# One kernel, a new opening: unit 0's v on another queue, weights behind a small write, products of zeros, and a new order of steps

## The chip, the cores and the metric

The kernel runs on one core of a Trainium2 chip. The core has five engines with an instruction queue each: TensorE (PE, matrix products, with its weight loads shown as PEld), VectorE (DVE), ScalarE (ACT), GpSimd (POOL) and SyncE (SP, which here only issues transfers). Transfers can be issued from SP, ACT and POOL; their packets are moved by 16 DMA engines that all queues share. Engines take their instructions strictly in the order of their own queue and wait for each other by semaphores.

The metric is device time in microseconds (us). The kernel before took 236.48 us, the median of 4 runs (235.59 to 236.83).

## The reference

For 4 batches, 8 heads, 768 time steps and a head size of 48, a gated linear recurrence and then a network with a rational activation:

```python
f = 1.0 / (1.0 + np.exp(-f_logit))
for t in range(S):
    state = f[:, :, t, :, None] * state + np.einsum('bhd,bhe->bhde', k[:, :, t], v[:, :, t])
    y[:, :, t] = np.einsum('bhd,bhde->bhe', q[:, :, t], state)
x = y.transpose(0, 2, 1, 3).reshape(B * S, H * D)      # 3072 x 384
h = x @ w_in                                           # 384 x 2048
P = a[0] + a[1] * h + a[2] * h * h + a[3] * h ** 3
Q = 1.0 + abs(b[0]) * abs(h) + abs(b[1]) * h * h
out = (P / (Q + 1e-6)) @ w_out                         # 2048 x 384
```

Inputs and the output are float32.

## The kernel before, in words

The work is cut into 12 units. Unit n is chunk n // 4 of 256 time steps and batch n % 4, with all 8 heads; units 0 to 3 are the first chunk, whose state starts at zero. A unit's 256 steps are two blocks (j = 0, 1) of 128.

The order of everything is written out by hand in one table, the string ORDER. Each entry names a step, its unit and its arguments; the program runs through the table once and issues what each step issues. So each engine's queue is the table filtered to that engine. A step that waits holds up all later steps of its engine. There is no scheduler behind the table. A number after @ names one of four PSUM slots, which the step takes over from its previous user, and for which it waits.

The steps of a unit, first the recurrence:

- `ld` loads f, k, q or v. f, k and q go through SP's queue in float32; v goes through POOL's queue, which converts it to bfloat16 on the way. Unit 0's f, k and q are loaded in two halves of four heads (arguments 2 4 and 0 2), the others in one piece. SP's transfers land in the order of issue.
- `ef`, `ls` (ACT): exp and log that make -log f. `cs` (PE): sums of it over time, by products with triangles of ones. `A` (ACT, line 312): the two exponentials of the sums; `xa` (DVE, line 317): q and k times them. `T` (PE, line 328) and `Te` (DVE, line 336): transposition and the copy out of PSUM.
- `sc` (PE, line 349) and `mk` (DVE, line 357): the masked scores of keys and queries. `ya` (PE): what the state gives to y, and the update of the state, which needs v; `ae` (ACT) and `st` (DVE): the new state. `vm` (line 364): two small copies of v into a padded tile. `yb` (PE, line 370): scores times v. `ye` (ACT, line 420): y out of PSUM.

Then the network, in groups of 128 of the 2048 columns, 0 to 16 (`h 0 4 8` is unit 0, groups 4 to 7):

- `h` (PE, line 438): y times w_in; `hy` (ACT, line 452): h to bfloat16; `ab` (DVE): its absolute value; `sq` (DVE) or `sa` (ACT): its square.
- Q: either `u` (PE, line 472), which adds the two terms by products with an identity, and `ln` (ACT, line 480) on the result in PSUM; or the sum in place by a DMA of POOL that accumulates (`zd`, line 489) or by DVE (`zv`), and `lz` (ACT, line 496) on the result. `ex` (ACT, line 504): 1/Q as the exponential of minus the logarithm.
- P: `p1`, `p2`, `pm` (DVE), and its last sum by an accumulating DMA of POOL (`ta`, line 523) or by DVE (`tv`). `gm` (DVE, line 532): P/Q.
- `o` (PE, line 539): the product with w_out; `oe` (ACT or DVE): out of PSUM; `so`, `s0`, `s1`: the store.

Once at the start: `wi` and `wo` load w_in and w_out through POOL's queue, four transfers for each `wi`, one per 32 partitions of the tile; `ab_` loads the coefficients a and b; `fa` and `fb` (DVE, lines 259 to 276) make scale factors from them, and `rg` reads two of these into registers of ACT, which `ye`, `ln` and `lz` use; `ca`, `cb`, `cc`, `cz` write constants. `zw` (zeros in a bfloat16 tile) and `wm` (products of that tile with itself into a PSUM slot that nobody reads) are defined in the program, but the table before does not use them.

In the table before, the coefficients are loaded by SP between unit 0's fourth and fifth half loads, and POOL issues v of unit 0 and then w_in's transfers as fast as it can.

## Time and profile before

One execution was profiled. It took 238.19 us, of which the program's span on the core is 236.5 us. The profile's numbers:

| engine | busy us | share of the span | instructions |
|---|---|---|---|
| PE | 215.6 | 91% | 3116 |
| DVE | 205.3 | 87% | 242 |
| ACT | 202.2 | 85% | 214 |
| POOL | 73.5 | 31% | 98 |

A line of the groups of instructions has the source line, the engine, the operation, what it writes and reads with the shape, how often, the busy time, the mean of one in ns, and the idle time of the engine just before it with what ended that. In a line of the time line, the first two numbers are the start and the duration in us; the bracket is the idle time of that engine before, and what ended it. In the table of stretches, each engine's busy us stand in the order PE, PEld, DVE, ACT, POOL, with the number of instructions, then TensorE's granted clock (1.00 is full speed), then the share of the DMA engines and the rate. In the chain of waits, a line has a start, a length and what the time went to.

A busy PE isn't PE at its peak: a product's end is modelled, and the same product takes longer with a slower clock.

### The profile page before, as it was taken

What the parts mean: (1) busy time and instruction counts of PE and PEld (TensorE: products, weight loads), DVE (VectorE), ACT (ScalarE), POOL (GpSimd) and SP (SyncE); (2) the same over time, 40 slices, a digit from 0 to 9 for tenths busy, and PEclk for the clock granted to TensorE, in tenths of its full rate; (3) what the DMA queues carried; (4) which work ended last, traced back from release to release, by engine and by line L of the source; (5) the groups of instructions that cost most, each with busy time, mean ns of one, the idle gap of its engine ahead of it and who ended that gap; (6) DMA issues with size and microseconds to landing.
All of it is one profiled execution on the core that took longest, in us unless ns stands there. A gap on an engine that the chain in (4) does not pass through costs nothing.

```text
span 236.5 us, 7112 instructions
## 1 busy us (share of the span) xinstructions
PE 215.6 (91%) x3116; PEld 148.6 (63%) x3128; DVE 205.3 (87%) x242; ACT 202.2 (85%) x214; POOL 73.5 (31%) x98
## 2 busy tenths in 40 slices
PE   1369779999999999999999999999999999999992
...
DVE  4653597899889899999999999999999799999940
ACT  5205584999997999999999999989999999899950
...
PEclk9999995999999999999999999999999999999999
...
GB/s 133 153 232 213 204 204 210 228 132 44 156 257 227 225 165 244 257 138 165 264 131 179 194 228 176 233 214 173 122 123 93 181 69 55 200 211 98 196 57 76
DMA packets 61998, 40.56 MB, mean 172 GB/s; under 512 B 51472, under 2 KB 58128, under 8 KB 61968
## 3 DMA queue, kind: packets, MB, share of 16 engines
...
q1 hardware_dynamic: 41104, 18.68, 33.1%
...
## 4 chain that ended last, share of the span: by engine, by line
PE 40%; DVE 20%; ACT 18%; DMA 12%; issue 6%; SPq 1%; DVEq 0%; POOLq 0%; ACTq 0%
PE op L539 13%; PE hp L438 12%; DMA z<-h 6%; ACT hy L452 5%; PE u L472 4%; DVE scm L357 4%; DMA kn<-in_k_dram 4%; ACT qi L504 3%; PE cs L303 3%; PE y L370 3%; ACT lq L496 2%; DVE gall L532 2%; DVE qkp L317 2%; DMA qn<-in_q_dram 2%; ACT lq L480 2%
## 5 line engine op out<-in xcount | busy, mean ns | idle before, releaser
L438 PE MATMUL hp<-xT,w_in_sb 128*128 128x256 bf16 x576 | 70.1, 278 | 1.6 <-DMA w_in_sb<-in_moe_w_in_dram 1.1
L539 PE MATMUL op<-w_out_sb,gall 128*128 128x384 bf16 x384 | 68.8, 326 | 0.6 <-DVE osb L554 0.6
L438 PEld LDWEIGHTS <-w_in_sb 128*128 128x128 bf16 x576 | 56.5, 100 | 12.1 <-issue 2.8
L452 ACT CAST hy<-hp 128x1024 bf16<-128x1024 f32 x48 | 49.3, 1067 | 4.8 <-PE hp L438 4.8
L539 PEld LDWEIGHTS <-gall 128*128 128x128 bf16 x384 | 36.4, 98 | 24.7 <-issue 1.1
L504 ACT ACTIVATE qi<-lq 128x2048 bf16<-128x2048 f32 (+1 forms) x25 | 46.8, 1879 | 0.1
L523 POOL DMA_DIRECT2D gall<-hy x21 | 18.6, 918 | 77.4 <-ACT lq L480 30.5
L532 DVE TENSOR_TENSOR gall<-gall,qi 128x2048 bf16<-128x2048 bf16 (+1 forms) x25 | 29.3, 1177 | 1.5 <-ACT qi L504 1.1
L519 DVE TENSOR_TENSOR gall<-gall,h 128x2048 bf16<-128x2048 bf16 (+1 forms) x25 | 29.2, 1175 | 0.0
L357 DVE TENSOR_TENSOR scm<-sc,mask 128x1024 bf16<-128x1024 f32 x24 | 29.0, 1215 | 0.3 <-PE sc L349 0.2
L480 ACT ACTIVATE lq<-u 128x1024 f32<-128x1024 f32 x24 | 24.6, 1050 | 1.8 <-PE u L472 1.8
L496 ACT ACTIVATE lq<-z 128x2048 f32<-128x2048 bf16 x12 | 23.6, 1969 | 1.5 <-DMA z<-h 1.5
L364 POOL COPY vmp<-vn 128x128 bf16<-128x128 bf16 x24 | 19.4, 897 | 15.8 <-PE y L370 6.3
L489 POOL DMA_DIRECT2D z<-h x9 | 12.1, 1347 | 38.4 <-DVE z L464 16.4
L456 DVE TENSOR_TENSOR h<-hy 128x2048 bf16<-128x2048 bf16 (+1 forms) x17 | 19.6, 1152 | 1.9 <-ACT hy L452 1.9
L312 ACT ACTIVATE A<-cs 128x768 f32<-128x768 f32 (+1 forms) x26 | 19.5, 800 | 1.6 <-PE cs L303 1.5
L317 DVE TENSOR_TENSOR qkp<-qn,A 128x768 bf16<-128x768 f32 (+1 forms) x13 | 11.7, 896 | 8.5 <-ACT A L312 8.1
L509 DVE TENSOR_SCALAR gall<-hy,a_sb 128x4096 bf16<-128x4096 bf16 (+2 forms) x15 | 17.1, 1140 | 2.1 <-ACT hy L452 2.1
L464 DVE TENSOR_SCALAR z<-hy 128x2048 uint16<-128x2048 uint16 (+1 forms) x25 | 17.0, 681 | 1.1 <-ACT hy L452 1.1
L460 ACT ACTIVATE h<-hp 128x1024 bf16<-128x1024 f32 x16 | 17.3, 1102 | 0.1
L303 PE MATMUL cs<-lsp,Ui 128*128 128x384 bf16 (+1 forms) x39 | 11.5, 360 | 5.9 <-ACT lsp L293 4.9
L328 PE MATMUL tp<-ident,qkp 128*128 128x128 bf16 x192 | 14.1, 227 | 3.0 <-DVE qkp L317 3.0
...
## 6 DMA issues: line engine op xcount, KB each, us to landing
...
```

What stands on the lines that cost most here:

```text
L312: nc.scalar.activation(t, src, AF.Exp, scale=1.0 if x else -1.0)
L357: nc.vector.tensor_mul(t, s["sc", g].rearrange("s r a i t -> s (r a) (i t)"), mb)
L364: nc.gpsimd.tensor_copy(s["vm"][:, :, :, 32 * x:32 * x + 16], src)
L438: nc.tensor.matmul(t[:, m - m0, :].rearrange("f (j t) -> f j t", j=UB), w_in_sb[:, kk, m * P:(m + 1) * P], s["x"][:, :, kk, :], start=(kk ...
L452: nc.scalar.copy(fl(big(s, "hy", "hy", 3), m0, m1), fl(s["hp", m0], 0, m1 - m0))
L456: nc.vector.tensor_mul(fl(big(s, "h2", "h2", 2), m0, m1), fl(s["hy"], m0, m1), fl(s["hy"], m0, m1))
L480: nc.scalar.activation(fl(s["lq", g], m0 - 8 * g, m1 - 8 * g), fl(s["u", m0], 0, m1 - m0), AF.Ln, scale=rsig2, bias=1.0 + 1e-6)
L496: nc.scalar.activation(fl(s["lq", g], m0 - 8 * g, m1 - 8 * g), fl(s["z"], m0, m1), AF.Ln, scale=rsig2, bias=1.0 + 1e-6)
L504: nc.scalar.activation(fl(s["qi", g], m0 - 8 * g, m1 - 8 * g), fl(s["lq", g], m0 - 8 * g, m1 - 8 * g), AF.Exp, scale=-1.0)
L519: nc.vector.tensor_mul(fl(s["g"], m0, m1), fl(s["g"], m0, m1), fl(s["h2"], m0, m1))
L532: nc.vector.tensor_mul(fl(s["g"], m0, m1), fl(s["g"], m0, m1), fl(s["qi", g], m0 - 8 * g, m1 - 8 * g))
L539: nc.tensor.matmul(s["op"][:, j, 0:DM], s["g"][:, m, C * j:C * j + C], w_out_sb[:, m, :], start=(m == 0), stop=(m == KF - 1))
```

## The change

The table is replaced. What it and the functions now do differently:

- Unit 0's v is loaded by SP in float32 as the seventh of its transfers, behind the six halves of f, q and k, into a tile of its own; a new step `vc` converts it on ACT. Unit 0's two `vm` copies are made by ACT. POOL loads v for the other units as before.
- The coefficients a and b are loaded through ACT's queue, at its head. `fa` and `fb` stand in DVE's queue ahead of all four of unit 0's `xa`; before, they stood between them. `rg` stands between unit 0's `A` steps.
- The half loads come as f, f, q, k, k, q; heads 4 to 7 go first through `xa`, `T` and `Te`.
- `hv` writes two zeros (bitcast to one float32) in each partition of w_in's tile, in group 0's columns, from DVE between the third and the fourth `xa` of unit 0. The load of groups 0 to 3 overwrites them, so it waits for that write, and what stands behind it in POOL's queue too: v of unit 1, groups 8 to 15 (now one `wi` with four transfers of double width), w_out. The load of groups 4 to 7 stands ahead of it and waits for nothing.
- 80 products of zeros (`wm`, 128x128 by 128x256) stand in 14 places of PE's queue, all before unit 0's `h 0 12 16`. In order of place there are 11, 1, 3, 5, 3, 6, 4, 2, 20, 5, 9, 1, 9 and 1 of them.
- After the start, the order of steps differs throughout. The set of steps is the same but for one half of a unit (8 groups), whose sum for Q is made by an accumulating DMA and one `lz`, where before two `u` and two `ln` made it: 22 `u` and `ln` instead of 24, 10 `zd` instead of 9, 13 `lz` instead of 12.

```diff
 ORDER = """
-cz 3; cb; ld 0 f 2 4; ld 0 f 0 2; ca; cz 2; ld 0 k 0 2; cz 0; ld 0 q 0 2; cz 1; ld 0 v; cc; ab_
-ef 0 2 4; wi 4 8; ls 0 2 4; ld 0 q 2 4; ef 0 0 2; cs 0 2 4 @0; ls 0 0 2; A 0 0 2 4; cs 0 0 2 @1
-ld 0 k 2 4; A 0 1 2 4; A 0 0 0 2; wi 0 4; ld 1 f; A 0 1 0 2; xa 0 0 0 2; fa; xa 0 1 0 2; rg; ld 1 q
-wi 12 16; fb; T 0 0 2 @1; xa 0 0 2 4; Te 0 0 2; ld 1 k; xa 0 1 2 4; sc 0 0 @1; ya 0 0 @0 @2; mk 0 0
-vm 0 1; ld 1 v; T 0 2 4 @3; ae 0; st 0 0; vm 0 0; Te 0 2 4; wi 8 12; ya 0 1; sc 0 1 @3; st 0 1
-yb 0 0 2; mk 0 1; ef 1; ld 2 f; ls 1; yb 0 2 4; ye 0; cs 1 @3; h 0 4 8 @0; A 1 1; A 1 0; ld 2 q
-h 0 0 4 @2; hy 0 4 8; xa 1 0; hy 0 0 4; sq 0 0 8; h 0 12 16 @2; wo 8 12; ld 2 k; xa 1 1; wo 4 8
-ab 0 0 8; wo 0 4; hy 0 12 16; T 1 @0; p1 0 0 8; wo 12 16; u 0 4 8 @3; Te 1; ef 2; ld 3 f; u 0 0 4 @2
-p2 0 0 8; ln 0 4 8; ld 2 v; ya 1 0 @0 @1; pm 0 0 8; ln 0 0 4; vm 1 0; sc 1 0 @3; vm 1 1; mk 1 0
-ae 1; ls 2; sc 1 1 @2; ld 3 q; ex 0 0 8; st 1 0; cs 2 @3; mk 1 1; ya 1 1; A 2 1; tv 0 0 8; yb 1
-A 2 0; h 0 8 12 @2; st 1 1; ye 1; ld 3 k; gm 0 0 8; h 1 4 8 @0; hy 0 8 12; xa 2 0; h 1 8 12 @2
-p1 0 8 16; hy 1 4 8; sq 0 8 16; sa 1 4 8; h 1 12 16 @1; xa 2 1; hy 1 8 12; h 1 0 4 @0; pm 0 8 16
-hy 1 12 16; ld 4 f; ef 3; T 2 @2; ab 0 8 16; hy 1 0 4; sq 1 8 16; u 0 8 12 @1; sa 1 0 4
-u 0 12 16 @3; p2 0 8 16; ln 0 8 12; ab 1 0 8; o 0 0 0 4 @0; tv 0 8 16; ln 0 12 16; u 1 4 8 @1; ls 3
...
+zw; ab_; cz 2; cb; ld 0 f 2 4; ld 0 f 0 2; ca; cz 3; ld 0 q 2 4; cz 1; ld 0 k 2 4; cz 0; cc
+ld 0 k 0 2; ef 0 2 4; ls 0 2 4; ld 0 q 0 2; ef 0 0 2; fa; wm 11 @3; cs 0 2 4 @0; ls 0 0 2; ld 0 v
+A 0 0 2 4; wm 1 @3; cs 0 0 2 @1; fb; A 0 1 2 4; xa 0 0 2 4; ld 1 f; rg; xa 0 1 2 4; A 0 0 0 2
+wm 3 @3; T 0 2 4 @0; A 0 1 0 2; ld 1 k; Te 0 2 4; xa 0 1 0 2; wm 5 @3; sc 0 1 @0; ld 1 q; hv 0
+xa 0 0 0 2; wi 4 8; mk 0 1; wm 3 @3; T 0 0 2 @1; vc 0; Te 0 0 2; vm 0 1 s; wm 6 @3; ya 0 0 @0 @2
+vm 0 0 s; wi 0 4; sc 0 0 @1; ae 0; ef 1; ld 2 f; st 0 0; mk 0 0; wm 4 @3; ya 0 1; ls 1; ld 1 v
+yb 0 2 4; st 0 1; yb 0 0 2; wi 8 16; cs 1 @1; ye 0; A 1 0; wm 2 @3; h 0 4 8 @0; A 1 1; hy 0 4 8
+xa 1 1; ld 2 k; wm 20 @3; h 0 0 4 @0; xa 1 0; ld 2 q; hy 0 0 4; wm 5 @3; T 1 @1; ab 0 0 8; sq 0 0 8
+ef 2; ld 3 f; Te 1; wm 9 @3; u 0 0 4 @0; ls 2; vm 1 1; ya 1 0 @2 @3; p1 0 0 8; vm 1 0; ln 0 0 4
+ld 2 v; cs 2 @1; p2 0 0 8; ae 1; sc 1 0 @0; st 1 0; A 2 1; ld 3 k; mk 1 0; wm 1 @0; ya 1 1; A 2 0
+xa 2 1; sc 1 1 @1; u 0 4 8 @0; st 1 1; mk 1 1; ln 0 4 8; ld 3 q; pm 0 0 8; ex 0 0 8; wm 9 @3; yb 1
+wm 1 @3; h 0 12 16 @1; wo 8 12; xa 2 0; ye 1; wo 0 4; tv 0 0 8; ld 4 f; h 0 8 12 @0; ef 3; wo 4 8
+gm 0 0 8; hy 0 12 16; wo 12 16; h 1 4 8 @2; hy 0 8 12; h 1 12 16 @1; ls 3; ld 4 k; sq 0 8 16
+sa 1 4 8; vm 2 1; h 1 8 12 @0; p1 0 8 16; hy 1 12 16; ld 3 v; ab 0 8 16; hy 1 4 8; h 1 0 4 @3
+vm 2 0; pm 0 8 16; hy 1 8 12; p2 0 8 16; u 0 12 16 @2; sa 1 0 4; ld 4 q; sq 1 8 16; u 0 8 12 @0
...
-u 10 8 12 @3; ex 10 0 8; pm 10 8 16; u 11 4 8 @2; o 9 0 8 12; pm 11 0 8; ta 10 8 16; ln 10 8 12
+h 11 0 4 @2; sq 10 8 16; ln 9 12 16; o 8 1 8 12; pm 10 0 8; zd 10 8 16; o 8 1 12 16; hy 11 0 4
...
@@ -190,12 +191,25 @@
         t0 = s["c"] * NT
         src, eng, dt = {"f": (f_logit, nc.sync, F32), "k": (k, nc.sync, F32),
                         "q": (q, nc.sync, F32), "v": (v, nc.gpsimd, BF16)}[what]
+        if n == 0 and what == "v":
+
+            what, eng, dt = "v32", nc.sync, F32
+            s[what] = consts.tile([P, H, 2, D], F32, name="v32")
         if what not in s:
             s[what] = ld.tile([P, H, 2, D], dt, name=what + "n")
         hh = slice(2 * a0, 2 * a1)
         eng.dma_start(out=s[what][:, hh].rearrange("p h i d -> p h (i d)"),
                       in_=src[s["b"], hh, t0:t0 + NT, :].rearrange("h (p i) d -> p h (i d)", i=2))
 
+    def vc(n):
+        s = unit(n)
+        s["v"] = ld.tile([P, H, 2, D], BF16, name="vn")
+        nc.scalar.copy(s["v"].rearrange("p h i d -> p (h i d)"), s["v32"].rearrange("p h i d -> p (h i d)"))
+
+    def hold(m0):
+
+        nc.vector.memset(w_in_sb[:, 0, m0 * P:m0 * P + 2].bitcast(F32), 0.0)
+
     def load_w_in(m0, m1):
 
         cols = slice(m0 * P, m1 * P)
@@ -208,9 +222,9 @@
                             in_=moe_w_out[m0 * P:m1 * P, :].rearrange("(ko ki) n -> ki ko n", ki=P))
 
     def load_ab():
-        nc.sync.dma_start(out=b_sb, in_=bass.AP(tensor=moe_b.tensor, offset=moe_b.offset,
+        nc.scalar.dma_start(out=b_sb, in_=bass.AP(tensor=moe_b.tensor, offset=moe_b.offset,
                                                 ap=[[0, P]] + list(moe_b.ap)))
-        nc.sync.dma_start(out=a_sb, in_=bass.AP(tensor=moe_a.tensor, offset=moe_a.offset,
+        nc.scalar.dma_start(out=a_sb, in_=bass.AP(tensor=moe_a.tensor, offset=moe_a.offset,
                                                 ap=[[0, P]] + list(moe_a.ap)))
 
     def const_a():
@@ -356,12 +370,16 @@
         mb = _at(mask, [[0, 4], [1, 2 * C]])
         nc.vector.tensor_mul(t, s["sc", g].rearrange("s r a i t -> s (r a) (i t)"), mb)
 
-    def vm(n, x):
+    def vm(n, x, eng="g"):
 
         s = unit(n)
         vv = s["v"].rearrange("p (a r) i d -> p r i a d", r=2)
         src = vv[:, 0, :, :, 32:48] if x == 0 else vv[:, 1, :, :, 0:16]
-        nc.gpsimd.tensor_copy(s["vm"][:, :, :, 32 * x:32 * x + 16], src)
+        dst = s["vm"][:, :, :, 32 * x:32 * x + 16]
+        if eng == "s":
+            nc.scalar.copy(dst, src)
+        else:
+            nc.gpsimd.tensor_copy(dst, src)
 
 
     PIECE = ((0, 0), (0, 1), (1, 1), (1, 2))
@@ -553,7 +571,7 @@
             s["osb"] = ms.tile([P, UB, DM], F32, name="osb")
         (nc.scalar.copy if eng == "s" else nc.vector.tensor_copy)(s["osb"][:, j0:j1], s["op"][:, j0:j1, 0:DM])
 
-    steps = dict(ld=load, wi=load_w_in, wo=load_w_out, ab_=load_ab, ca=const_a, cb=const_b, cc=const_c,
+    steps = dict(ld=load, hv=hold, vc=vc, wi=load_w_in, wo=load_w_out, ab_=load_ab, ca=const_a, cb=const_b, cc=const_c,
                  cz=const_z, fa=coef_a, fb=coef_b, rg=regs, wm=wm, zw=zero_w, ef=ef, ls=ls, cs=cs, A=A, xa=xa, T=T, Te=Te,
                  sc=sc, mk=mk, vm=vm, ya=ya, yb=yb, ye=ye, ae=ae, st=st, h=h, hy=hy, sq=sq, ab=ab, u=u, ln=ln,
                  zv=zv, zd=zd, sa=sa, lz=lz, ex=ex, p1=p1, p2=p2, pm=pm, ta=ta, tv=tv, gm=gm, o=o, oe=oe, so=store,
```

## The prediction

> **What bounds the kernel now.** I read the slices of the page first, then the stretches of the start and of the middle, then the chain of waits and the time line up to 45 us.
>
> The page's slices (40 of 5.9 us each, busy tenths):
>
> ```profile
> PE   1369779999999999999999999999999999999992
> DVE  4653597899889899999999999999999799999940
> ACT  5205584999997999999999999989999999899950
> PEclk9999995999999999999999999999999999999999
> ```
>
> The stretches:
>
> ```profile
> 12.00:18.00 6.00, 4.19 (x78) 3.08 (x78) 3.05 (x5) 0.77 (x2) 5.33 (x11) 1.00 1.20 232
> 18.00:24.00 6.00, 5.65 (x93) 3.66 (x93) 1.78 (x2) 3.22 (x5) 2.98 (x5) 1.00 1.35 213
> 36.00:42.00 6.00, 6.00 (x115) 4.31 (x115) 3.93 (x5) 3.04 (x4) 0.00 (x0) 0.57 1.14 204
> 80.00:220.00 140.00, 139.06 (x2118) 98.39 (x2124) 136.63 (x141) 138.10 (x141) 44.63 (x47) 1.00 0.89 171
> ```
>
> From 80 to 220 us PE idles 0.9 us, ACT 1.9 and DVE 3.4: all three are full, and a us gained ahead of this stays gained. The slack is in the first 42 us. There, the chain of waits:
>
> ```profile
> 4.44 9.05 DMA kn<-in_k_dram
> ...
> 18.94 1.24 DVE scm L357
> ...
> 22.65 3.38 PE hp L438 x24
> ```
>
> And the time line:
>
> ```profile
> 7.89 0.17 DVE L259 TENSOR_SCALAR bm<-b_sb 128x2 uint32<-128x2 uint32 x1 [0.28 <-DMA b_sb<-in_moe_b_dram]
> ...
> 13.52 0.56 DVE L317 TENSOR_TENSOR qkp<-kn,A 128x384 bf16<-128x384 f32 x1 [1.41 <-DMA kn<-in_k_dram]
> ...
> 21.30 0.81 ACT L420 ACTIVATE xT<-y 128x768 bf16<-128x768 f32 x1 [2.17 <-PE y L370]
> ...
> 22.44 1.83 PE L438 MATMUL hp<-xT,w_in_sb 128*128 128x256 bf16 x8
> ...
> 27.12 1.47 PE L438 MATMUL hp<-xT,w_in_sb 128*128 128x256 bf16 x12 [1.10 <-DMA w_in_sb<-in_moe_w_in_dram]
> ...
> 41.28 1.01 ACT L452 CAST hy<-hp 128x1024 bf16<-128x1024 f32 x1 [1.83 <-PE hp L438]
> ...
> 43.05 1.22 DVE L456 TENSOR_TENSOR h<-hy 128x2048 bf16<-128x2048 bf16 x1
> ```
>
> The last half of k is issued at 4.44 and lands at 13.5; unit 0 ends with `ye` at 22.1. The 128x256 product takes 0.229 us at 22.44 and 0.122 at 27.12, though the granted clock is written as 1.00 in both: I read the early rows as half speed, not yet on record. It is on record for 36 to 42 us (0.57).
>
> **The change, part by part.** Landings below are issue plus time to landing.
>
> *Loads.* In SP's queue the first four half loads land at 3.6, 4.3, 5.4 and 6.0 us, then b at 7.9, a at 8.8, and the fifth and sixth half at 10.95 and 13.5. So b and a, 3 KB, stand in front of q and k for some 2.5 us, and v and seven w_in transfers of POOL run beside the last two halves. Now b and a are on ACT's queue, and POOL starts with four w_in transfers. At 0.8 us per half, six halves land by 7.6; v (two halves) by 9.2, plus four w_in transfers at 0.65 each (their landings follow each other so) 11.8. Bounds for v: 9.2 and 13.5 (the sixth half of before); I take 11.8. `vc` is a 128x768 pass on ACT, 0.84, and two `vm` there 0.2 to 0.5 each (POOL's rows 0.30): v is ready at 13.2. It is covered if `ya 0 0` can't start sooner.
>
> The Trainium skill speaks against this part: "DMA: Bandwidth & Descriptors", section "Issuing engines are not separate DMA queues", says that issuing from several engines saves only issue time. By that rule moving b and a gains about 1 us (two issues of 0.43 to 0.51). The 7.0 and 9.1 us to landing of the halves behind them, against 3.6 ahead, say more.
>
> *b at the head of DVE.* `fa` (7.89 to 9.39, 1.5 us) and `fb` (0.7) now precede all `xa`, so b's landing heads the chain. ACT issues it after its table load, at 2.1. With the 4.9 us to landing of before it is there at 7.0, with the 2.4 of ACT's store at 4.5; I take 6.0, as half of its old wait was for the loads ahead of it. ACT's two issues (0.5 each) end at 3.1, before f lands; `rg` waits for `fa` (7.5) and holds two `A` of 0.49, which end at 8.6, 2 us before their `xa`. Then `fa`, `fb` to 8.2; two `xa` of 0.56 to 9.3; `T` to 9.9; `Te` 0.69 to 10.6; two `xa` and `hv` (0.1) to 11.8; `T` 0.7 to 12.5; six zeros of 0.23 to 13.9 (covering v); `ya 0 0` 1.4 to 15.3; `ae` and `st` 0.9 to 16.2; `ya 0 1` from 16.8 (behind `sc` 0.64 and four zeros 0.9) to 18.3, with `mk` 1.22 beside it; `yb` 2.1 to 20.4; `ye` 0.8 to 21.2, against 22.1: 0.9 gained with the slow clock throughout. With the fast one after 12 us the zeros, `ya`, `yb` give up half: 0.7 + 0.7 + 0.45 + 0.7 + 1.0 = 3.5, so 4.4 gained. With half of the stretch fast, `ye` ends at 19.4 and 2.7 is gained.
>
> The zeros stand in gaps of PE; a gap that closes early turns them into a delay, 0.12 us each fast, 0.23 slow (the same shape). The skill's "TensorE: Matmul & The Clock Gate", section "The HAM clock gate (the 'warmup' mystery)", has full speed after about 3.4 us of sustained products. By that alone it would come before 12 us and the gain would be the 4.4. This trace has products for 5.65 of 6 us from 18 to 24 and yet 0.229 us at 22.44; I stay between.
>
> *From `ye` to unit 0's last square.* `A 1` two times 0.76 on ACT to 20.9; `h 0 4 8` (12 products, 1.4) on PE to 20.8; `hy` to 21.9. Then 20 zeros, 2.4 us, to 23.2, `h 0 0 4` to 24.6, `hy` to 25.6. The held w_in transfers (issued from about 11.4 to 13.7, 5.5 to 9.0 to landing as before) are in by 17 to 22.7, so the zeros, not the weights, set this. Behind them in POOL's queue stand v of unit 1 (issued at 14.5; 9.7 to landing before, so 24, wanted by `ya 1 0` at 28), and w_out behind the copies of that v (issued to 27; up to 15.5 to landing, so 42.5, wanted by `o` past 43). `ab`, `sq`, `Te 1` (0.69, 1.23, 1.22) to 28.7, against 31.65. `p1`, `p2`, `st` to 30.9, `mk` 32.1, `xa` 33.1; on PE `ya 1 1` and `sc 1 1` behind a zero that waits for that `mk`'s slot, to 33.5; `u` 0.9 to 34.4; on ACT `ln` 0.96, `ex` 1.92, `ye 1` 0.81, `ef 3` 0.85 and two `hy` to 41.0. Before, `hy 0 8 12` ends at 42.3 with `ef 3` (0.88) still to do: ACT is 2.2 ahead. `sq 0 8 16` ends at 42.2 against 44.27, with an `xa` (0.95) more and a `p1` (0.81) less behind it: DVE too is 2.2 ahead. The old slow stretch from 34 to 41 has no place in this chain: nine zeros and `yb` precede `h 0 12 16`. `ef 3` needs f of unit 3, which landed at 42.9 before and wasn't needed till 46.2; now SP's queue carries one more load but loses its block, and POOL's transfers start later. If it landed at 40 the chain would wait 2 us.
>
> *The full middle.* Two `u` and two `ln` less, one `zd` and one `lz` more. PE: 8 products of 128x512, at 0.215, are 1.7 us less. ACT: 2 x 1.05 - 1.97 = 0.1 less. POOL: 1.35 more, hidden in its 31%; the accumulation lands in 7.0. As all three engines are full, between 0.1 and 1.7 is gained; at the end PE has 8 us of `op` products without a pause from 222, so I take the middle, 0.9. The new order there can't be priced from the diff: it can save at most ACT's 1.9 us of idle time, and I let it cost up to DVE's 3.4 once more; value 0, as ends of both signs are near.
>
> Sum: 2.2 + 0.9 = 3.1. The profiled execution goes from 238.19 to 235.1; it stood 0.7% above the median, from which 236.48 - 3.1 = **233.4 us**.
>
> **Rivals.**
> - *The zeros lie on the chain and open no clock* (slower). Place: the 20 before `h 0 0 4`. At the slow clock, with `ye` at 21.2, `h` (2.75), 20 zeros (4.6) and `h` again (2.75) end at 31.5, `hy`, `ab`, `sq`, `Te` at 35.7: 4.0 behind 31.65, so 240.5 less the 0.9: 239.6. It decides if the slow clock holds beyond about 26 us. Against it: 24 `hp` products sufficed before.
> - *Held weights late* (slower). The point is 23.2, where the zeros end; each us beyond it costs one, and beyond 26.5 the start gains nothing. At 9.0 to landing they are in by 22.7. Wide transfers for groups 8 to 15 are wanted only at 35; v before had up to 16.0 to landing, from 18 at the latest: 34. A transfer 3.5 us later still: 238.
> - *The start's gain is given back* (no change): unit 3's f at 40 takes 2 of the 2.2; or a queue in the middle stands behind an accumulation not yet landed (before: 1.5 us over two such waits for `z`). 235.5 to 237.
> - *Clock open by 12 us and PE the bound*: 4.4 + 1.7 = 6.1, so 230.4.
>
> **How the numbers follow.** Forecast 0.64, open clock 0.08, given back 0.16, zeros 0.08, weights 0.04. The forecast's own range is 231.0 to 235.2. Of "given back" I count 0.02 as faster and 0.03 as slower: faster by over 0.5% (1.2 us, about what a measurement of this kernel can tell) 0.74, same 0.11, slower 0.15. The range cuts half of the fast case, and most of the two slow ones: 230.8 to 237.8.
>
> **What would show it.** b lands by 7 us, and the line 259 starts there; q and k of unit 0 land by 8, v by 12; `ye` ends between 18 and 21; the 12 products of `h 0 4 8` take about 1.4 us; `h 0 0 4` follows the zeros with no wait for w_in; ACT's `ef 1` and `ef 2` don't wait for f, and `ef 3` starts by 39; `sq 0 8 16` ends near 42; between 80 us and 217 all three engines idle as little as before. I am wrong if b lands after 8, if the first `hp` products still take 0.23, if ACT waits for f of unit 2 or 3, or if the middle shows new waits for `z` or `gall` of over 2 us.

## The result, and the profile after

The changed kernel takes as long as the kernel before: its time over that of the kernel before is 0.999, with a 95% interval from 0.9966 to 1.0013 (medians 237.67 us over 42 runs and 237.22 over 63). The forecast was 233.4 us, 3.1 less. The profiled execution went from 238.19 to 237.28 us, its span from 236.5 to 235.6. Ratios are taken over undisturbed runs only, the medians over all; the profiled execution after is 1.5% above its kernel's fastest run and so not an undisturbed one, but the start that it shows is there again in e3 and its wait for z in e6, whose profiled executions are.

The slices of the page after (40 of 5.9 us, busy tenths):

```profile
PE   5778869999999999999999999979999999999991
DVE  6573579699999979999999999979999999999960
ACT  3455257999996999999999999969999999999970
PEclk9999997999999999999999999999999999999999
```

TensorE is busier in the first three slices, which hold the zero products. PE, DVE and ACT now all have a notch in slice 27 (153 to 159 us), where PE and DVE stood at 9 and ACT at 8 before. The stretches after (columns: length, busy time of PE, its weight loads, DVE, ACT, POOL, then granted clock, DMA share, GB/s):

```profile
12.00:18.00 6.00, 4.58 (x148) 3.56 (x150) 4.47 (x6) 3.08 (x6) 4.96 (x9) 1.00 1.13 221
18.00:24.00 6.00, 5.21 (x61) 4.17 (x50) 1.93 (x3) 3.24 (x4) 0.78 (x3) 1.00 1.31 205
36.00:42.00 6.00, 6.00 (x103) 4.62 (x102) 4.63 (x5) 5.11 (x5) 0.00 (x0) 0.85 1.30 200
80.00:220.00 140.00, 137.35 (x2110) 97.43 (x2115) 135.05 (x138) 137.00 (x136) 42.07 (x45) 1.00 0.91 171
```

From 80 to 220 us PE idles 2.65 us where it idled 0.94, DVE 4.95 (3.37) and ACT 3.0 (1.9). So less work was put into a middle that also waits more. The slow clock from 36 to 42 us is shorter (0.85, not 0.57), but it is still there.

The chain of waits after (start, length, what):

```profile
13.75 15.00 DMA fn<-in_f_logit_dram
...
39.23 7.86 PE hp L456 x72
...
142.74 1.32 POOL vmp L382
144.91 10.40 DMA z<-h
155.33 1.91 ACT lq L514
```

Two transfers are now on the chain. One is unit 2's f, from its issue by SP at 13.75 to its landing at 28.75. The other is unit 6's accumulation into z, issued by POOL at 144.91 behind copies of v, and landed at 155.3. The time line shows what waits for them:

```profile
4.07 0.29 DVE L273 TENSOR_SCALAR bm<-b_sb 128x2 uint32<-128x2 uint32 x1 [0.39 <-DMA b_sb<-in_moe_b_dram]
...
6.58 0.52 ACT L302 ACTIVATE fn<-fn 128x384 f32<-128x384 f32 x1 [1.20 <-DMA fn<-in_f_logit_dram]
...
13.81 0.83 ACT L207 CAST vn<-v 128x768 bf16<-128x768 f32 x1 [4.40 <-DMA v<-in_v_dram]
...
18.32 0.81 ACT L438 ACTIVATE xT<-y 128x768 bf16<-128x768 f32 x1 [0.92 <-PE y L388]
...
19.18 1.14 PE L456 MATMUL hp<-xT,w_in_sb 128*128 128x256 bf16 x9
...
28.78 0.84 ACT L302 ACTIVATE fn<-fn 128x768 f32<-128x768 f32 x1 [2.63 <-DMA fn<-in_f_logit_dram]
...
36.62 1.73 PE L298 MATMUL wm<-zw 128*128 128x256 bf16 x9
36.86 1.02 ACT L498 ACTIVATE lq<-u 128x1024 f32<-128x1024 f32 x1 [3.95 <-PE u L490]
...
43.10 1.22 DVE L474 TENSOR_TENSOR h<-hy 128x2048 bf16<-128x2048 bf16 x1 [2.02 <-ACT hy L470]
```

Unit 0's `ye` ends at 19.13, 3.0 us ahead of the 22.11 of before, and the first `hp` products take 0.127 us each, not 0.229. By 43.10, where unit 0's last square starts (43.05 before), nothing of this lead is left: ACT waits 2.63 us for f of unit 2, then 3.95 for `u` (32.9 to 36.9), the last 2.5 of them at the half clock that lasts from 34.4 to 37.8, and nine zeros stand at 36.62 ahead of unit 1's `yb`. The whole gain of 0.9 us in the span comes after 43 us.

### The profile page after: what moved, and what is told of

It reads as the page before. It is cut to its first block, busy times and chain, and to the rows that moved or that the text cites. A ratio compares the mean times of both kernels' runs of the same rounds, so it can differ in the third digit from the quotient of the medians.

```text
span 235.6 us, 7258 instructions
## 1 busy us (share of the span) xinstructions
PE 218.3 (93%) x3188; PEld 152.9 (65%) x3200; DVE 205.8 (87%) x244; ACT 203.0 (86%) x216; POOL 68.1 (29%) x92
## 3 DMA queue, kind: packets, MB, share of 16 engines
HBM read 25.17 MB, written 4.72 MB: 127 GB/s over the span
## 4 chain that ended last, share of the span: by engine, by line
PE 55%; DVE 17%; DMA 17%; issue 4%; SPq 3%; ACT 2%; POOL 1%; POOLq 0%; DVEq 0%; ACTq 0%
PE op L557 18%; PE hp L456 17%; DMA fn<-in_f_logit_dram 9%; PE u L490 7%; DMA z<-h 4%; DMA gall<-hy 4%; DVE gall L537 3%; PE y L388 3%; SPq L201 3%; DVE scm L371 3%; PE tp L342 2%; PE sc L363 2%; PE sv L411 2%; DVE gall L550 1%; PE cs L317 1%
## 5 line engine op out<-in xcount | busy, mean ns | idle before, releaser
L557 PE MATMUL op<-w_out_sb,gall 128*128 128x384 bf16 x384 | 69.7, 326 | 0.6 <-DVE osb L572 0.6
L456 PE MATMUL hp<-xT,w_in_sb 128*128 128x256 bf16 x576 | 67.3, 273 | 0.8 <-issue 0.8
L557 PEld LDWEIGHTS <-gall 128*128 128x128 bf16 x384 | 36.0, 98 | 23.5 <-issue 0.9
L541 POOL DMA_DIRECT2D gall<-hy x21 | 20.7, 1034 | 70.0 <-ACT alast L443 25.6
L514 ACT ACTIVATE lq<-z 128x2048 f32<-128x2048 bf16 x13 | 25.3, 1948 | 2.1 <-DMA z<-h 2.1
L498 ACT ACTIVATE lq<-u 128x1024 f32<-128x1024 f32 x22 | 22.2, 1058 | 5.5 <-PE u L490 5.5
L382 POOL COPY vmp<-vn 128x128 bf16<-128x128 bf16 x22 | 16.0, 760 | 35.2 <-PE y L388 14.2
L507 POOL DMA_DIRECT2D z<-h x10 | 9.6, 956 | 35.6 <-ACT hy L470 13.8
L532 DVE TENSOR_SCALAR hy<-hy,a_sb 128x4096 bf16<-128x4096 bf16 (+2 forms) x15 | 16.9, 1128 | 0.1
L298 PE MATMUL wm<-zw 128*128 128x256 bf16 x80 | 13.6, 316 | 2.4 <-DVE scm L371 1.4
L302 ACT ACTIVATE fn<-fn 128x768 f32<-128x768 f32 (+1 forms) x13 | 10.6, 816 | 6.0 <-DMA fn<-in_f_logit_dram 6.0
```

Of the source, the lines that this page charges most:

```text
L456: nc.tensor.matmul(t[:, m - m0, :].rearrange("f (j t) -> f j t", j=UB), w_in_sb[:, kk, m * P:(m + 1) * P], s["x"][:, :, kk, :], start=(kk ...
L498: nc.scalar.activation(fl(s["lq", g], m0 - 8 * g, m1 - 8 * g), fl(s["u", m0], 0, m1 - m0), AF.Ln, scale=rsig2, bias=1.0 + 1e-6)
L514: nc.scalar.activation(fl(s["lq", g], m0 - 8 * g, m1 - 8 * g), fl(s["z"], m0, m1), AF.Ln, scale=rsig2, bias=1.0 + 1e-6)
L541: nc.gpsimd.dma_start(out=fl(s["g"], m0, m1), in_=fl(s["hy"], m0, m1), accum_op=ALU.add)
L557: nc.tensor.matmul(s["op"][:, j, 0:DM], s["g"][:, m, C * j:C * j + C], w_out_sb[:, m, :], start=(m == 0), stop=(m == KF - 1))
```

## The experiments

To read them I cut each trace at four ends: that of unit 0's `ye`; that of the fourth `hy` (`hy 0 8 12`, which ends the start); those of the `ye` of units 7 and 8; and that of ACT's last `osb`. "Slow" is the time at half clock between 18 and 42 us, from the granted clock of the stretches (for example 0.87 and 0.85 over 6 us each are (0.13 + 0.15) x 6 / 0.5 = 3.4 us). It comes in steps of 3.4 us. The profile has no record of the clock before it first opens, and that time isn't in the column: the first record of the full clock starts at 8.0 to 13.5 us in the kernels with the early zeros, but at 23.5 in e9, and at 20.9 to 27.9 in those without zeros.

| kernel | `ye` of unit 0 | exp of unit 2's f | slow | fourth `hy` | to `ye` 7 | `ye` 7 to 8 | `ye` 8 to `osb` | ratio to before, 95% |
|---|---|---|---|---|---|---|---|---|
| before | 22.11 | 31.39 | 6.8 | 42.29 | 100.47 | 17.06 | 72.94 | 1 |
| after | 19.13 | 29.62 | 3.4 | 43.07 | 98.50 | 19.02 | 71.30 | 0.999, 0.997 to 1.001 |
| e1_no_zeros | 20.43 | 29.49 | 0 | 41.15 | 98.47 | 18.61 | 71.54 | 0.995, 0.991 to 0.998 |
| e2_hold_more | 18.69 | 27.21 | 0 | 41.77 | 99.04 | 19.01 | 71.30 | 0.992, 0.987 to 0.996 |
| e3_zd_first | 19.12 | 29.12 | 6.8 | 43.59 | 98.72 | 16.70 | 71.57 | 0.998, 0.994 to 1.003 |
| e4_before_ab | 21.79 | 30.39 | 3.4 | 40.92 | 101.54 | 16.31 | 73.16 | 0.990, 0.985 to 0.995 |
| e5_three | 20.40 | 27.49 | 10.2 | 43.13 | 98.55 | 16.68 | 71.59 | 0.988, 0.980 to 0.995 |
| e6_ab_late | 19.20 | 28.47 | 3.4 | 43.23 | 98.62 | 18.85 | 71.33 | 1.001, 0.997 to 1.005 |
| e7_before_u10 | 22.71 | 32.40 | 3.4 | 41.95 | 100.46 | 17.07 | 73.26 | 1.006, 1.002 to 1.010 |
| e8_v_pool | 18.43 | 26.66 | 0 | 40.94 | 99.27 | 16.80 | 71.58 | 0.993, 0.987 to 0.998 |
| e9_no_hold | 23.32 | 32.42 | 3.4 | 48.03 | 98.35 | 19.04 | 71.37 | 1.012, 1.007 to 1.018 |
| e10_pool_zd | 17.95 | 25.89 | 6.8 | 42.42 | 99.36 | 16.68 | 71.58 | 0.985, 0.978 to 0.991 |
| e11_pool_zd_nozeros | 19.41 | 26.29 | 3.4 | 40.56 | 98.46 | 16.69 | 71.81 | 0.983, 0.979 to 0.988 |
| e12_pool_ab | 19.54 | 27.74 | 3.4 | 42.08 | 98.56 | 16.81 | 71.79 | 0.995, 0.991 to 0.999 |
| e13_before_vsp | 25.17 | 33.84 | 3.4 | 44.38 | 100.47 | 16.58 | 72.96 | 1.008, 1.003 to 1.012 |
| e14_u10_back | 19.19 | 26.50 | 10.2 | 41.92 | 98.61 | 16.69 | 73.30 | 0.988, 0.984 to 0.991 |
| e15_pool_hold | 18.50 | 26.92 | 6.8 | 43.30 | 98.68 | 18.93 | 71.30 | 0.999, 0.995 to 1.003 |
| e16_early_zeros | 18.45 | 26.50 | 3.4 | 39.47 | 98.45 | 16.71 | 72.71 | 0.992, 0.987 to 0.996 |

Four pairs of kernels are alike until long after the start and differ up to there in the clock alone: e8 and e10, after and e3 (until unit 6's accumulation), e11 and e14, e7 and before (until unit 10). Their fourth `hy` ends at 40.94 and 42.42, with two steps of slow time between them; at 43.07 and 43.59, with one; at 40.56 and 41.92, with two; and at 41.95 and 42.29, with one. So 3.4 us at half clock cost 0.3 to 0.7 us up to there. I take 0.7, from the two pairs that are two steps apart, and "like for like" below means the fourth `hy` less 0.7 us per step. Within such a pair `ye` of unit 0 still differs by up to 0.6 us (22.11 and 22.71), so a difference of less than that between two traces shows nothing by itself. In e6 and e12 one more step began before 18 us (at 15.5 and 14.9) and is not in the column.

### The four parts that I suspected first

e1 leaves out all 80 zero products (every `wm` step). e2 lets unit 2's loads past the weights, with a second hold. e3 puts unit 6's accumulation ahead of unit 9's copies on POOL. e4 is the kernel before with b and a on ACT's queue and nothing else.

```diff
# e2
-yb 0 0 2; wi 8 16; cs 1 @1; ye 0
+yb 0 0 2; cs 1 @1; ye 0
-h 0 0 4 @0; xa 1 0; ld 2 q
+h 0 0 4 @0; xa 1 0; hv 8; wi 8 16; ld 2 q
# e3
-vm 9 0; ab 6 0 8; o 4 1 12 16
+ab 6 0 8; zd 6 0 8; vm 9 0; o 4 1 12 16
# e4, on the kernel before
-cz 3; cb; ld 0 f 2 4
+ab_; cz 3; cb; ld 0 f 2 4
-        nc.sync.dma_start(out=b_sb, in_=bass.AP(tensor=moe_b.tensor, offset=moe_b.offset,
+        nc.scalar.dma_start(out=b_sb, in_=bass.AP(tensor=moe_b.tensor, offset=moe_b.offset,
-        nc.sync.dma_start(out=a_sb, in_=bass.AP(tensor=moe_a.tensor, offset=moe_a.offset,
+        nc.scalar.dma_start(out=a_sb, in_=bass.AP(tensor=moe_a.tensor, offset=moe_a.offset,
```

> The changed kernel without its 80 products of zeros; nothing else is touched. Theory A (the start's gain is real and is given back between 28 and 43 us, at the landing of unit 2's f and at a slow stretch of TensorE): the zeros brought the fast clock at 10.5 us, without them it comes at 20 to 24 us, ye of unit 0 ends 1 to 2 us later (20 to 21 instead of 19.1), but h 0 0 4 starts at once, 2 us sooner against its h 0 4 8; f of unit 2 lands at 28.8 as before, so the square of the second half of unit 0 still ends at 43 to 45 and the time is within 1 us of the changed kernel, 236 to 238. Theory B (the zeros themselves cost the gain, as they stand ahead of real products): the square ends near 41 and the time falls to about 235. Theory C (the zeros pay): the time rises to 239 or more, with a slow clock in the granted clock's rows up to 40 us.

> The changed kernel with a second small write, into w_in's group 8, behind the q product of unit 1 on VectorE, and the load of groups 8 to 15 behind it; so 1.6 MB of weights leave the queues between 18 and 27 us to f, k and q of units 1 and 2. Theory A (unit 2's f, landing at 28.8, holds ScalarE and so the state, the scores, u and the square): f of unit 2 lands at 23 to 25, the ACT wait of 2.6 us on it is gone, the square of unit 0's second half ends at 41 to 42 instead of 44.3, w_in's groups 8 to 15 land at 33 to 36, in time for 37. The time falls by 1 to 2 us if the middle carries it, to 235 to 236. Theory B (what the start gains is lost in the middle whatever the start does): the start shows the same gain and the time stays within 0.5 us. Theory C: the weights now come late, h 0 12 16 waits for w_in and the time rises by 1 or more.

> The changed kernel with one accumulating transfer of unit 6 (groups 0 to 7, the sum for Q) moved in GpSimd's queue ahead of the two v copies of unit 9 and the load of unit 10's v, behind which it was issued at 144.9 us and landed at 155.3, while ScalarE waited 2.1 us for it and VectorE and TensorE behind that 1.6 to 1.7 us each. Theory A (this wait is where the middle gives back what the lesser TensorE work gains): it is issued 3 to 4 us sooner, lands by 151 to 152, the three waits go, and the time falls by 1 to 2 us, to 235 to 236.5. Theory B (the middle is full, and the time that is freed here shows up as another wait, since VectorE bounds the middle and it had only 1.7 us of idle time there): less than 0.7 us.

> The kernel before with one part of the change: the coefficients a and b by ScalarE's queue, at its head, instead of in SP's queue between the fourth and the fifth half load. If the small transfers stood in front of q and k, as the prediction had it, the fifth and sixth half load land 2 to 2.5 us sooner (8.5 to 9 and 11 to 11.5 instead of 10.95 and 13.5), and ye of unit 0 ends 1 to 2 us sooner, at 20 to 21. If the page's rule holds that another issuing queue saves only issue time, they land 1 us sooner. For the time: theory A (a gain of the start is given back before 43 us at transfers) 236 to 237.5, no change; if the start's gain is carried to the end, 1 to 2 us less.

*e1.* Without zeros unit 0's `ye` is 1.3 us later, the trace's first full clock comes at 20.9 us and not at 10.5, and the start still ends earlier: 41.15 against 43.07, or 42.37 like for like. So the zeros win 1.3 us at `ye` and cost 1.2 net by the end of the start; what they do to the slow time itself is left out of this. The wait for f of unit 2 stays, as theory A said; but unit 0's last square starts at 41.18 and the time falls by 0.4% (0.995 against 0.999, with intervals that just overlap), so theory B is the nearer one, at less than its size.

*e2.* Unit 2's f is exponentiated 2.4 us earlier and ACT no longer waits for it; the start ends at 41.77, 0.6 ahead of the changed kernel like for like. So in this trace the 2.63 us wait was worth about a quarter of its length: behind it ACT still waits 1.72 and 2.77 us for `u`. The ratio, 0.992 against 0.999, is some 1.7 us, theory A's size; where the rest of it comes from the trace doesn't show, as the wait for z stays too (19.01).

*e3.* The time line of POOL and of ACT in e3:

```profile
142.01 0.86 POOL L507 DMA_DIRECT2D z<-h  x1 [4.00 <-ACT qi L522]
142.55 2.09 POOL L382 COPY vmp<-vn 128x128 bf16<-128x128 bf16 x2
```

```profile
153.69 1.98 ACT L514 ACTIVATE lq<-z 128x2048 f32<-128x2048 bf16 x1
```

The accumulation is issued ahead of the two copies, 2.9 us earlier than in the changed kernel, and `lq` starts without a wait. The stretch from `ye` 7 to `ye` 8 falls from 19.02 to 16.70 us: the new order's wait for z cost 2.3 us there. The ratio alone (0.998 against 0.999) doesn't show it: by the time theory B holds, by this stretch theory A. The profile has 6.8 us of slow clock against 3.4; whether the timed runs lose the gain in the same way is open.

*e4.* Stretches (the last two numbers are the DMA engines' share and GB/s) of the changed kernel, of e6 (below), where b and a come later, and of the kernel before:

```profile
2.00:4.50 2.50, 1.59 (x8) 0.95 (x7) 1.96 (x14) 0.29 (x2) 2.36 (x7) 1.00 0.61 121
```

```profile
2.00:4.50 2.50, 1.59 (x8) 0.95 (x7) 1.57 (x12) 0.99 (x3) 2.36 (x7) 1.00 0.95 240
```

```profile
5.50:7.50 2.00, 0.83 (x5) 0.40 (x3) 0.44 (x1) 1.81 (x5) 2.00 (x5) 1.00 0.30 24
```

With b and a at the head of ACT's queue the loads beside them move at half the rate (121 GB/s against 240; e4 has 121 too); in SP's queue, as before, they hold up what stands behind them almost fully (24 GB/s). In e4 the second exp of unit 0's f comes at 6.48 where it came at 4.59, and `ye` ends at 21.79 against 22.11. So the move shifted the stall from q and k to f, and of the 2.5 us that I read from the landings 0.3 remain at `ye`, less than like kernels differ there. The time says more: the ratio of 0.990 (0.985 to 0.995) belongs to this edit alone, as nothing else differs. The medians, 236.07 and 237.16 us, are 0.5% apart, and the trace's last `osb` ends 0.85 us earlier. How much the move is worth to the whole, and by what way, is not shown.

### Combined, and each part undone

e5 is e1, e2 and e3 together. e6 issues b and a by SP behind unit 0's v and puts their steps later. e7 is the kernel before with only unit 10's products replaced by an accumulation. e8 undoes v's move: POOL loads it in bf16 again, nothing is held, and the copies are POOL's.

```diff
# e6, on the changed kernel (b and a by nc.sync)
-zw; ab_; cz 2
+zw; cz 2
-ls 0 0 2; ld 0 v
+ls 0 0 2; ld 0 v; ab_
# and fa behind "mk 0 0", fb behind "st 0 1", rg ahead of "ye 0"
# e7, on the kernel before
-zd 10 0 8; ex 9 0 8
+zd 10 0 8; zd 10 8 16; ex 9 0 8
-u 10 12 16 @3; p1 11 8 12
+p1 11 8 12
-ln 10 12 16
-u 10 8 12 @3; ex 10 0 8
+ex 10 0 8
-ln 10 8 12
+lz 10 8 16
# e8, on the changed kernel
-        if n == 0 and what == "v":
+        if False:
-hv 0
-vc 0
-vm 0 1 s
+vm 0 1
-vm 0 0 s
+vm 0 0
```

> The changed kernel without its zero products, with unit 2's loads let past the weights (a second hold, weights 8 to 16 behind it), and with unit 6's low accumulation ahead of unit 9's copies on POOL. Theory A (the start's gain is given back at unit 2's f, at the closed clock and at unit 6's accumulation): the three repairs touch different waits, so their ratios multiply, 0.995 x 0.992 x 0.998 = 0.985 of the kernel before, about 233.5 us; no wait for fn of unit 2 over 0.5 us on ACT, no wait of lq for z over 1 us near 155 us, and no granted clock under 0.95 after 24 us. Rival (only the granted clock between 30 and 42 us differs from run to run, and the three singles each drew a lucky one): no better than the singles, about 236 us, ratio 0.993 to 0.998.

> The changed kernel with the two small transfers b and a issued by SP behind unit 0's v, and the coefficients' steps behind unit 0's masks. Theory A (the two transfers stall whatever is loaded beside them; at the head of ACT's queue they stall unit 0's f): the first two exps of f start again at 3.6 and 4.6 us (4.30 and 6.58 in the changed kernel), unit 0's xT ends 1 to 1.5 us earlier (about 18), and the total stays within 0.5% of the changed kernel, since unit 2's f still lands late (28 to 29 us) and takes it. Rival one (the f halves are late for another reason, such as zeros or SP's issue): exps still at 4.3 and 6.6. Rival two (the start's gain reaches the end): about 1.3 us less than the changed kernel, ratio 0.994.

> The kernel before with one part of the change alone: the high half of unit 10's denominator is summed by an accumulating DMA (zd, lz) and not by eight products on PE. My prediction took 0.9 us for it, between nothing and PE's 1.7 us. Theory A (the full middle takes PE's 1.7 us as far as PE bounds it, and the loss of the changed kernel lies elsewhere): 0.4 to 1.0 us less, ratio 0.996 to 0.998, with PE's busy time after 200 us down by 1.6 to 1.8 us. Rival (so near the end the accumulation's 7 to 10 us until it lands are waited for): no change or slower, ACT's lq waits for z of unit 10 over 1 us, ratio 0.999 to 1.005.

> The changed kernel with unit 0's v by POOL's casting transfer as before, no cast on ACT, the vm copies on POOL and no held weights; zeros, a/b on ACT's queue and the rest of the table as changed. Theory A (only what unit 1 and 2 meet later sets the time, the start itself is not worth more than what is given back): v usable at 11 to 13 us, the half loads late by what the weights take (last xa of unit 0 after 14), unit 0's xT 1 to 3 us later than the changed kernel's 19.1, unit 2's f earlier than its 28.8, the total within 0.5% of the changed kernel. Rival (v by SP and the held weights carry a gain that the rest loses): 1 to 3 us slower than the changed kernel, ratio over 1.005.

*e5.* 0.988 with 10.2 us of slow clock in its profile: this is near the 0.985 that theory A had from the single parts, but the interval (0.980 to 0.995) reaches into the rival's range too, and theory A's claim that the clock would stay open fell. Like for like the start ends at 41.0, and the z wait is gone (16.68).

*e6.* ACT's time line of e6:

```profile
4.56 0.51 ACT L302 ACTIVATE fn<-fn 128x384 f32<-128x384 f32 x1
...
18.39 0.81 ACT L438 ACTIVATE xT<-y 128x768 bf16<-128x768 f32 x1 [2.03 <-DVE a_sb L290]
```

With b and a late, the second f is there at 4.56, without a wait: the transfers were what had held it. But `ye` now waits 2.03 us for the coefficients, since I placed their steps between unit 0's masks and its states. Up to 15 us everything is 0.7 to 2 us earlier, and the total is the same (1.001): as theory A said, though part of the reason is my placing. e12 tries a better one.

*e7.* PE's busy time from 200 to 234 us, of the kernel before and of e7:

```profile
200.00:234.00 34.00, 31.33 (x297) 19.41 (x297) 26.95 (x34) 27.32 (x25) 4.22 (x5) 1.00 0.71 146
```

```profile
200.00:234.00 34.00, 29.93 (x288) 18.20 (x289) 26.70 (x34) 27.06 (x24) 5.10 (x6) 1.00 0.79 159
```

PE has 1.4 us less to do and the end doesn't move: 73.26 us from `ye` 8 to the last `osb` against 72.94, and a ratio of 1.006. My 0.9 us for this part is nothing in the old order, or less: theory A is wrong. The rival's wait of `lq` for z of unit 10 is not there either, so what takes the place of PE's 1.4 us is not shown.

*e8.* POOL's and ACT's time line of e8:

```profile
11.79 0.52 POOL L382 COPY vmp<-vn 128x128 bf16<-128x128 bf16 x2 [5.43 <-DMA vn<-in_v_dram]
```

```profile
25.81 0.85 ACT L302 ACTIVATE fn<-fn 128x768 f32<-128x768 f32 x1
```

By POOL's queue v is there at 11.8 us, in bf16; by SP's it landed at 13.8 and needed the cast. `ye` ends 0.7 us earlier, f of unit 2 is there without a wait, and the start ends at 40.94, 1.4 us earlier like for like. The rival of this run was wrong, and so was theory A's later `ye`: v's move together with its hold is a loss. In this profile the z wait didn't occur either (16.80), with the changed kernel's order on POOL; e15 has it again (18.93). In e8 the two copies of v ahead of the accumulation took 1.39 us and it was issued at 141.10, in the changed kernel 3.84 and at 144.91. So whether the wait bites differs between kernels with the same order there, and by what is not shown.

### v's way and the hold apart

e9 leaves out only the hold, e15 only v's move (POOL loads it, the hold stays), and e13 makes only v's move in the kernel before (`ld 0 v` by SP behind the half loads, a cast on ACT ahead of unit 0's last `xa`).

```diff
# e9
-hv 0
# e13, on the kernel before
-ld 0 k 2 4; A 0 1 2 4
+ld 0 k 2 4; ld 0 v; A 0 1 2 4
-A 0 1 0 2; xa 0 0 0 2
+A 0 1 0 2; vc 0; xa 0 0 0 2
```

> The changed kernel without the small write that holds the weights; unit 0's v stays on SP's queue with its cast on ACT. Theory A (the held weights are still moving when unit 2's f is to be loaded, and that is where the start's gain is given back): unit 2's f lands 2 to 3 us earlier (its exp ends at 26.5 to 27.7, against 29.6 in the changed kernel and 26.7 with v by POOL and no hold), the half loads and v come 1 to 2 us later, and the total falls by 1 to 2 us, ratio 0.990 to 0.996. Rival (it is v's way by SP, ACT's cast and ACT's two copies that cost, not the hold): exp of unit 2's f still past 29, the total as the changed kernel, ratio 0.997 to 1.002.

> The kernel before with one part of the change alone: unit 0's v is loaded in full precision by SP behind the half loads and cast on ACT; nothing is held, and POOL's copies stay. Theory A (v's 1024 packets in SP's queue move every later load of units 1 and 2 back by 1.4 to 2.3 us, and nothing pays for it as the weights share the engines): unit 2's exp of f ends 1 to 3 us later than the 31.4 of the kernel before, the total 1 to 3 us more, ratio 1.004 to 1.013. Rival (v by SP lands sooner than by POOL and is worth it): unit 0's xT earlier than 22.1, ratio 0.990 to 0.998.

> The changed kernel with unit 0's v by POOL's casting transfer, and the hold kept. Theory A (v in SP's queue is the loss, the hold by itself is harmless once v is not there): unit 0's xT within 0.5 us of the 18.4 that v by POOL without a hold gave, unit 2's exp of f ends at 26 to 27.5, the total within 0.4% of that run, ratio 0.989 to 0.996. Rival (the hold is the loss, and with v on SP it only costs less than it saves): unit 0's first products wait for the weights or unit 2's f ends past 28.5; ratio 0.996 to 1.004.

ACT's and DVE's time line of e9, and ACT's of e13:

```profile
15.97 0.83 ACT L207 CAST vn<-v 128x768 bf16<-128x768 f32 x1 [6.53 <-DMA v<-in_v_dram]
...
45.38 0.84 ACT L302 ACTIVATE fn<-fn 128x768 f32<-128x768 f32 x1 [1.97 <-DMA fn<-in_f_logit_dram]
```

```profile
25.42 0.96 DVE L331 TENSOR_TENSOR qkp<-kn,A 128x768 bf16<-128x768 f32 x1 [3.76 <-DMA kn<-in_k_dram]
```

```profile
16.09 0.83 ACT L206 CAST vn<-v 128x768 bf16<-128x768 f32 x1 [8.69 <-DMA v<-in_v_dram]
```

With v on SP and the weights let go (e9, and e13 in the old order), v lands at 16 us, and f, k and q of units 1, 2 and 3 are each late: the start ends at 48.0 and 44.4. My theory for e9 was the wrong way round; beside v on SP the hold is what makes v's move bearable. Part of e9's loss is the clock, which opens only at 23.5. With v on POOL the hold costs: e15 ends the start at 41.9 like for like, e8 at 40.9. Traces with equal slow time say the same without a correction: e3 (v on SP, hold) 43.59, e15 (v on POOL, hold) 43.30, e10 (v on POOL, no hold) 42.42. So of the 1.2 us between e3 and e10, 0.9 stand with the hold, and the 0.3 that stand with v's move are within what like kernels differ by. e15 has f of unit 2 as early as e8 (26.9), and its total is still that of the changed kernel (0.999); its profile has both the z wait and 6.8 us of slow clock. So my theory A for e15 got its milestones, and the total is its rival's.

e13 came out as its theory A had it, in unit 2's f (33.84 against 31.39) and in the total (1.008).

### On the better start

e10 is e8 with e3's order, e11 is e10 without zeros, e12 is e10 with b and a behind unit 1's f and their steps in DVE's gaps, e14 is e11 with unit 10's eight products back on PE, e16 is e10 with only the 33 zeros ahead of unit 0's `ye`.

```diff
# e12, on e10 (b and a by nc.sync)
-xa 0 0 2 4; ld 1 f; rg; xa 0 1 2 4
+xa 0 0 2 4; ld 1 f; ab_; xa 0 1 2 4
# and fa behind "Te 0 0 2", fb behind "st 0 1", rg ahead of "ye 0"
# e14, on e11
-zd 10 8 16
+u 10 12 16 @2; ln 10 12 16; u 10 8 12 @2
-lz 10 8 16
+ln 10 8 12
# e16, on e10: behind "ye 0" every wm step is left out
-wm 2 @3; wm 20 @3; wm 5 @3; wm 9 @3; wm 1 @0; wm 9 @3; wm 1 @3
```

> The changed kernel with unit 0's v by POOL, no hold, and unit 6's low accumulation ahead of unit 9's copies. Theory A (the wait for unit 6's sum costs 1.5 us wherever it is met): since the run with v by POOL alone showed no wait of lq for z near 155 us, the reorder has little left to gain there, 0 to 0.5 us less than that run: ratio 0.990 to 0.993. Rival (the reorder is worth its full 1.5 us through POOL's later work): ratio 0.985 to 0.988.

> The same as e10 without the zero products. Theory A (the zeros open the clock some 10 us earlier, which saves 1 to 1.5 us up to unit 0's xT, but stand in PE's queue ahead of products that set the end, and an early opened clock closes once more often): within 0.3% of e10, with unit 0's xT 1 to 1.5 us later. Rival one (the zeros pay): 0.4 to 1% slower than e10. Rival two (the zeros cost, as their removal alone suggested with 0.9946 against the changed kernel's 0.999): 0.3 to 0.6% faster than e10.

> The same as e10 with the two small transfers by SP behind unit 1's f and the coefficients' steps in DVE's gaps (behind unit 0's second Te and behind its second state). Theory A (these transfers stall whatever is loaded beside them; once nothing urgent is beside them, the start is earlier by what they cost): exps of unit 0's f start at 3.6 and 4.6, unit 0's xT ends 1 to 1.5 us before that of e10 (17.4 at best), and unit 1's xT about as much; total 0.5 to 1.2 us less than e10. Rival (unit 1's loads then land later and take it, as when they were moved late with v on SP): xT of unit 1 as in e10, total within 0.2% of e10.

> The kernel e11 (v by POOL, no hold, unit 6's accumulation first, no zeros) with unit 10's eight products back on PE and its accumulating transfer gone. Theory A (near the end PE's 1.7 us are no bound, as the kernel before with that part alone showed): up to 190 us as e11 but for a constant, and from there to the end a change between -0.4 and +0.4 us; ratio as e11's 0.983 within 0.2%. Rival (in the changed order the term is worth the 0.9 us that I took): the stretch from 190 us to the end 0.6 to 1.7 us longer than in e11, ratio about 0.987.

> The same as e10 (v by POOL, no hold, unit 6's accumulation first) with only the 33 zero products ahead of unit 0's ye; the 47 behind it are left out. Theory A (the early zeros open the clock and are the gain, the late ones stand on the chain and are the cost): unit 0's xT ends at 18.0 to 18.5 as with all zeros, the fourth hy 1.0 to 1.7 us earlier than in e11 once the same length of slow clock is counted (39.8 there), the total at e11's ratio of 0.983 or below, 0.977 to 0.983. Rival one (the late zeros keep the clock open through unit 1's gaps, and what they cost is paid back): two or more slow stretches of 3.4 us between 20 and 42 us in the profile, ratio 0.985 to 0.990. Rival two (neither matters beyond the spread): fourth hy as in e11, ratio 0.982 to 0.985.

*e10.* In the profile e3's order adds 0.1 us to e8, which had no z wait to lose (16.68 against 16.80): theory A. The ratio, 0.985, is the rival's, but its interval reaches to 0.991 and overlaps that of e8.

*e11* is the best version that I ran: 0.983 (0.979 to 0.988), 4.0 us (0.017 x 237) less than the kernel before, and about as much less than the changed one. Against e10 the start ends 1.2 us earlier like for like (39.86 against 41.02), the second pair in which the zeros cost more than they save; in total the two can't be told apart.

*e12.* b lands late and stops DVE at 13.5, and `ye` comes at 19.54, 1.6 later than in e10. Its trace has 6.8 us of slow clock from 14.9 to 21.7, after the clock had been open from 8.0. 0.995, 1% worse than e10, where theory A had a gain and the rival no change: both are wrong, and of the places that I tried for the two small transfers none is better than the head of ACT's queue.

*e14.* ACT's time line of e11 and of e14 (`xT` is unit 8's, `osb` the last):

```profile
154.89 0.81 ACT L437 ACTIVATE xT<-y 128x768 bf16<-128x768 f32 x1
...
227.04 0.48 ACT L571 COPY osb<-op 128x384 f32<-128x384 f32 x1 [3.63 <-PE op L556]
```

```profile
156.41 0.81 ACT L437 ACTIVATE xT<-y 128x768 bf16<-128x768 f32 x1
...
230.04 0.48 ACT L571 COPY osb<-op 128x384 f32<-128x384 f32 x1 [3.52 <-PE op L556]
```

Up to unit 8 e14 follows e11 at a constant distance; from there, at full clock in both, it takes 73.30 us against 71.81, 1.5 more. Its ratio is 0.988 against 0.983, with intervals that overlap. The five kernels that have these products on PE, or the old order, take 72.9 to 73.3 us there, twelve of the thirteen others 71.3 to 71.8 (the last, e16 below, 72.7). So in the changed order unit 10's products are worth nearly PE's whole 1.7 us. Theory A, taken over from e7, is wrong here, and the rival right.

*e16.* Stretch of e16, and ACT's line behind it:

```profile
24.00:30.00 6.00, 4.68 (x52) 3.21 (x51) 4.17 (x5) 3.69 (x5) 4.42 (x7) 0.74 1.26 238
```

```profile
33.25 1.02 ACT L497 ACTIVATE lq<-u 128x1024 f32<-128x1024 f32 x1 [1.50 <-PE u L489]
```

`ye` comes as early as with all zeros (18.45), and the fourth `hy` at 39.47, 38.8 like for like, the earliest of all. So the early zeros are the gain at `ye` and the late ones the cost up to the end of the start, as theory A said. But the time did not follow: 0.992, worse than theory A's bound of 0.983, and beyond rival one's range too. The medians of e16 and e11, 234.22 and 232.93 us, are 0.5% apart and their ratios 0.9%, so part of that distance lies in the runs of the kernel before that each was compared with. Over its timed runs the mean granted clock is lower than e10's (it answers to 2.3 slow steps a run, from the clock and span of each, against 1.6), which speaks for rival one, that the late zeros keep the clock open; the profiled run had one step. In that run the lead over e11, 1.09 us at unit 8's `ye`, is gone at unit 9's (170.80 and 170.76). PE's time line of e16 has one idle time between them that e11 hasn't:

```profile
155.25 0.38 PE L489 MATMUL u<-z,ident 128*128 128x512 bf16 x1 [0.98 <-issue]
```

"issue" is time in which the engine waited for nothing that the profile shows. Whether it is there by chance, and whether the clock is what holds the timed runs back, is left open.

## Why the prediction was wrong, step by step

**The full middle: right in kind, undersized.** I took 0.9 us for unit 10's products and 0 for the new order, 0.9 together. The profiles show 100.47 + 17.06 + 72.94 = 190.47 us from the fourth `hy` to the last `osb` before, and 98.50 + 19.02 + 71.30 = 188.82 after: 1.65 less. It is made of -1.97 up to unit 7 (the new order, just past my bound of -1.9), +1.96 between units 7 and 8 (the z wait, 2.3 by e3), and -1.64 behind unit 8 (unit 10's products, 1.5 by e14). The size of that last term depends on the order: by e7 it is nothing in the old one.

**Loads and b: the step failed, and its error was covered.** I had q and k of unit 0 land by 7.6 and v by 11.8. The last q came at 12.55 and v at 13.8, 5 and 2 us later. What I read as a block in SP's queue alone is also a stall of what moves beside the two small transfers on another queue (121 GB/s against 240). b itself came at 4.07, ahead of my 6.0 and of the lower bound of 4.5. I weighed the Trainium skill, "DMA: Bandwidth & Descriptors", section "Issuing engines are not separate DMA queues", against it and decided against it: it allowed about 1 us and I took more. At `ye` e4 measured 0.3, nearer the page than me; over the whole time its ratio says 1.2 to 3.6 us, so e4 doesn't decide between the page and me.

**`ye` of unit 0: the number was right for the wrong reasons.** I took 19.4; it ended at 19.13. The loads were 2 to 5 us later than I had them, and the clock opened earlier: the trace's first full clock comes at 10.5 us, the first `hp` products take 0.127 us. On this the other rule that I weighed, in "TensorE: Matmul & The Clock Gate", section "The HAM clock gate (the 'warmup' mystery)", was also nearer than my "between": with zeros in the gaps the changed kernel's clock opened before 12 us. That is no rule for zeros in gaps, though. In the changed kernel products follow each other without a gap from 7.71 us and the clock opens at 10.5; in e9, with the same zeros, they do so from 7.73 to 12.4, and it opens at 23.5.

**From `ye` to unit 0's last square: the step that failed.** I let 2.2 us of the lead reach 43 us; 0.0 did, and like for like the changed kernel's fourth `hy` is 1.5 us behind the kernel before (42.37 against 40.89). Three terms of it were wrong. First, I wrote that the slow stretch "has no place in this chain"; the changed kernel's profile has 3.4 us of it, at 34.4, and e3's, which has the same start, 6.8. Zeros don't prevent it. Second, I took the zeros behind `ye` as fillers of gaps; by e1, and by e10 against e11, all zeros together cost 1.2 us at the end of the start although they gain 1.3 to 1.5 at `ye`, and e16 places the cost on those behind `ye`. Third, I priced v's move by v's landing alone. I named SP's one load more, and set no price on it, and none on the hold: f of unit 2 landed at 28.8 and was waited for 2.63 us, and v's move with its hold is a loss of 1.4 us by e8 and of 1.2 by e3 and e10, of which 0.9 to 1.0 stand with the hold (e15 against e10 and e8). Undone together, with the wait for z (e11), they bring the time from 0.999 to 0.983, with intervals far apart. But these terms are not all of it. Even e11, without zeros, with v on POOL and no hold, has 2.7 us of lead at `ye` and 1.0 like for like at the fourth `hy`; where those 1.7 us go, no run here takes apart.

**The rivals.** "The start's gain is given back" is what happened, and both of its places were the right kind: f of a later unit (unit 2's, where I named unit 3's) and a queue behind an accumulation that had not landed. I gave it 0.16. It deserved more, as each of its parts is a separate way to lose, and I had read from the first 42 us only what was ahead of the new chain, not what was next to end last. Held weights weren't late: `h 0 0 4` starts at 23.62, right behind the zeros. The zeros did lie on the chain, as that rival had it, but in the changed kernel they opened the clock. (That rival's sum is 0.2 us too high: 21.2 + 2.75 + 4.6 + 2.75 is 31.3.) The condition of the last rival, a clock open by 12 us, came true, and its gain did not: with late loads `ye` came at 19.13, not at the 17.7 of its 4.4 us, and the lead was lost behind it.

**The signs that I named.** b after 8: no. First products at 0.23: no. ACT waits for f of unit 2 or 3: yes, 2.63 us. New waits for z over 2 us: yes by the letter, one of 2.09 us, where before had 0.71 and 0.80; behind it VectorE and TensorE waited 1.58 and 1.67. Two of four came true.
